# Group 3's keys and queries through TensorE instead of the DMA crossbar, and two loads issued ahead of the index tables

## The chip, the cores and the metric

The kernel runs on one core of a Trainium2 chip. The metric is the device time of one execution in microseconds (us); the kernel before takes 244.34 us (median of 3 runs, 244.31 to 244.9). The profile is one further execution, whose span from the first to the last instruction is 242.5 us.

The engines are named as in the profile: PE is TensorE (PEld its weight load), DVE is VectorE, ACT is ScalarE, POOL is GpSimd, SP is SyncE. POOLq and SPq stand for the issuing of transfers from these engines.

## The reference

Attention with a sliding window and sink positions, then a gated feed-forward block on its output. Four batches, eight heads, 768 positions, head size 64; each query sees itself, the 127 positions before it, and the first four positions (the sinks).

```python
scores = scale * np.matmul(q, k.transpose(0, 1, 3, 2))
keep = is_sink | in_window            # is_sink: pos < 4; in_window: 0 <= rel < 128
scores = np.where(keep, scores, -1000000000.0)
a = softmax(scores)                   # written out in the original
attn_out = np.matmul(a, v)
x = attn_out.transpose(0, 2, 1, 3).reshape(3072, 512)
g = x @ w_gate                        # 512 x 1536
silu = g * (1.0 / (1.0 + np.exp(-g)))
out = (silu * (x @ w_val)) @ w_out    # 1536 x 512
```

## The kernel before

The 3072 positions are cut into 12 groups of 256 (three groups in a batch). For each group keys and queries have to be brought from rows by position to columns by position (feature on partitions)[...]. The kernel does that in three ways: groups 0 and 1 by matmuls on specially packed rows, group 2 by TensorE transposes (`step_TN`), groups 3 to 11 by the DMA crossbar (`xbar`), from the queue of SyncE:

```python
rowp = pool("rowp", 3)
natp = pool("natp", 1)
...
def load_nat(g):
    b, c = divmod(g, GC)
    x = (natp if g > 2 else rowp).tile(
        [P, 2, 2, DM], BF16, tag="nat" if g > 2 else "rows", name="nat")
    for i, src in ((0, k), (1, q)):
        for j in range(2):
            t0 = c * 256 + j * P
            nc.gpsimd.dma_start(
                x[:, i, j].rearrange("p (h d) -> p h d", d=D),
                src[b, :, t0:t0 + P].rearrange("h p d -> p h d"))
    nats[g] = x
...
def step_TN(g, i, j):
    ...
    pt = bank([P, NP2, P], BF16, "pn")
    for p in range(NP2):
        nc.tensor.transpose(pt[:, p], nats[g][:, i, j, p * P:(p + 1) * P], ident)
    ...
    if i == 0:
        nc.scalar.copy(out=dst, in_=pt)
    else:
        nc.vector.tensor_copy(out=dst, in_=pt)

def xbar(g):
    ...
    for j in range(2):
        for i in range(2):
            t0 = c * 256 + j * P
            nc.sync.dma_start_transpose(
                (kTs, qTs)[i][b][:, :, t0:t0 + P], nats[g][:, i, j])
```

From group 3 on the blocks share `natp`, which holds one buffer: a group's block can be loaded only when the crossbar has read the one before it. The pool `rowp` has three buffers; the two fp32 staging tiles of the start and group 1's rows take them first.

GpSimd issues all loads of keys, queries, values and weights, in this order (cut):

```python
nc.gpsimd.iota(tq, ...)      # index tables: 0..127 along a row
nc.gpsimd.iota(tk, ...)      # 0..127 down the partitions
nc.gpsimd.iota(th8, ...)
for i in range(2):
    nc.gpsimd.dma_start(x0[:, i, 4:8], by_two((k, q)[i], 4))
load_rows(1)
load_v(0)
load_gate(0)
...                          # gates 1 and 2, values 1, group 2's block, gate 3, values 2, gates 4, 5
for i in range(4):
    load_out(i)
...
load_nat(3)
load_v(3)
```

Attention work is woven into the feed-forward work of the groups before it. `gate` projects with both weight matrices (`pg`, `pv`), `down` with the output weights (`pd`); a slot number says at which gate or down step an attention step stands, after `pg` and before `pv`. This is the first stage (slots 0 to 17 are gates, 18 to 23 downs):

```python
(11, [A(xbar, 3)]), (11, [NV(4)]),
(15, [A(xbar, 4)]), (15, [NV(5)]), (19, [A(xbar, 5)]), (19, [NV(6)]),
(23, [A(xbar, 6)]), (23, [NV(7)]),
((17, 18), Ss(3)), (18, [A(step_ks, 1)]), (18, [A(step_vsb, 1)]),
((19, 19, 19, 20), PVs(3)), (20, Xs(3)),
((19, 20), Ss(4)), (19, [K(4)]),
((21, 21, 22, 22), PVs(4)), (22, Xs(4))))
```

`NV(g)` loads group g's block and values, `Ss` computes scores, exponentials and masks, `K` the scores against the sinks, `PVs` the products with the values, `Xs` brings the normalised rows (`xn`) into columns (`xT`) for the gates: for groups 0, 1, 2 and 4 by TensorE, for the others by the crossbar.

At the start VectorE makes the identity and the masks from the index tables, before its first casts:

```python
nc.vector.tensor_scalar(ident, tq, tk, None, op0=ALU.is_equal)
...                                          # two halves of mask
nc.vector.tensor_scalar(sk, tk, float(NS), None, op0=ALU.is_lt)
...                                          # mask0: mask with the sinks let through
nc.vector.tensor_scalar(lt8, th8, float(NS), None, op0=ALU.is_lt)
...                                          # diag_h: which row belongs to which head's sinks
```

Of the kernel before, what the change touches and what calls it, by code (L numbers as in the profile page):

```python
# [8 lines left out]
BF16 = mybir.dt.bfloat16  # L9
AF = mybir.ActivationFunctionType  # L10
ALU = mybir.AluOpType
# [3 lines left out]
def kernel(  # L15
# [12 lines left out]
    nc = tc.nc  # L28
    P = 128
    B, H, S, D = q.shape  # L30
    NS = int(n_sink)
    W = int(window)
    DM = moe_w_gate.shape[0]
# [19 lines left out]
    def pool(name, bufs, psum=False):  # L53
        if psum:
            return ctx.enter_context(
                tc.tile_pool(name=name, bufs=bufs, space=bass.MemoryType.PSUM))
        return ctx.enter_context(tc.tile_pool(name=name, bufs=bufs))
# [3 lines left out]
    rowp = pool("rowp", 3)  # L61
    natp = pool("natp", 1)
# [15 lines left out]
    def bank(shape, dtype, name):  # L78
        return psum.tile(shape, dtype, tag="b", name=name)


    rows, nats, vas = {}, {}, {}

    def by_rows(src, b, w, pairs, t0):

        hs = slice(2 * pairs.start + w, 2 * pairs.stop, 2)
        return src[b, hs, t0:t0 + 256].rearrange("p (m r) d -> m p (r d)", r=4)
# [3 lines left out]
    def new_rows(g):  # L91
        rows[g] = rowp.tile([P, 2, NP2, 4 * D], BF16, tag="rows", name="rows")
        return rows[g]

    def load_rows(g):
        b, c = divmod(g, GC)
        x = new_rows(g)
        for i in range(2):
            for w in range(2):
                nc.gpsimd.dma_start(  # L100
                    x[64 * w:64 * (w + 1), i],
                    by_rows((k, q)[i], b, w, ALL, c * 256))

    def load_nat(g):
        b, c = divmod(g, GC)
        x = (natp if g > 2 else rowp).tile(
            [P, 2, 2, DM], BF16, tag="nat" if g > 2 else "rows", name="nat")
        for i, src in ((0, k), (1, q)):
            for j in range(2):
                t0 = c * 256 + j * P  # L110
# [5 lines that stand above are left out]
    def load_v(g):  # L116
        b, c = divmod(g, GC)
        va = vpool.tile([P, 2, H, VS], BF16, tag=f"va{g}", name="va")
        nc.vector.memset(va[:, :, :, D:D + 1], 1.0)
# [3 lines that stand above are left out]
                va[:, j, :, 0:D], v[b, :, t0:t0 + P].rearrange("h p d -> p h d"))  # L123
        vas[g] = va
# [3 lines left out]
    def load_gate(i, which=(0, 1)):  # L128
        f0, n = sum(FCH[:i]) * P, FCH[i] * P
        both = (wgs, moe_w_gate, "wg"), (wvs, moe_w_val, "wv")  # L130
        for lst, w, nm in (both[x] for x in which):
            t = wpool.tile([P, DMC, n], BF16, tag=f"{nm}{i}", name=nm)
            nc.gpsimd.dma_start(  # L133
                t, w[:, f0:f0 + n].rearrange("(c p) f -> p c f", p=P))
            lst.append(t)
# [9 lines left out]
    mask = const.tile([P, 2, 256], BF16)  # L145
    mask0 = const.tile([P, 2, 256], BF16)
    diag_h = const.tile([P, 4], BF16)
    vcf = const.tile([P, B, D + 1], FP32)
    tq = const.tile([P, P], FP32)
    tk = const.tile([P, 1], FP32)  # L150
    th8 = const.tile([P, 4, 4], FP32)
    lt8 = const.tile([P, 4, 4], FP32)
    sk = const.tile([P, 1], FP32)
# [15 lines left out]
    def by_two(src, h0):  # L169
        return src[0, h0:h0 + 4, 0:256].rearrange("h (m r) d -> m h (r d)", r=2)  # L170

    x0 = const.tile([P, 2, H, 2 * D], BF16)
# [5 lines left out]
    for h in range(H):  # L178
        r = 32 * (h // 4) + NS * (h % 4)
        nc.sync.dma_start(  # L180
            vcf[r:r + NS, :, 0:D], v[:, h, 0:NS].rearrange("b s d -> s b d"))
    nc.gpsimd.iota(tq, [[1, P]], base=0, channel_multiplier=0,
                   allow_small_or_imprecise_dtypes=True)
    nc.gpsimd.iota(tk, [[0, 1]], base=0, channel_multiplier=1,
                   allow_small_or_imprecise_dtypes=True)
    nc.gpsimd.iota(th8, [[-32, 4], [-NS, 4]], base=0, channel_multiplier=1,
                   allow_small_or_imprecise_dtypes=True)
    for i in range(2):
        nc.gpsimd.dma_start(x0[:, i, 4:8], by_two((k, q)[i], 4))
    load_rows(1)  # L190
    load_v(0)
    load_gate(0)
    load_gate(1, (0,))
    load_v(1)
# [8 lines left out]
    for i in range(4):  # L203
# [3 lines left out]
    tq2 = tq.rearrange("p (o x) -> p o x", o=1).broadcast_to([P, 2, P])  # L207
    nc.vector.tensor_scalar(mask[:, :, 0:P], tq2, tk, None, op0=ALU.is_lt)
    nc.vector.tensor_scalar(mask[:, :, P:2 * P], tq2, tk, None, op0=ALU.is_ge)
    nc.vector.tensor_scalar(sk, tk, float(NS), None, op0=ALU.is_lt)  # L210
    flat, flat0 = (m.rearrange("p a x -> p (a x)") for m in (mask, mask0))
    nc.vector.tensor_scalar(flat0[:, P:3 * P], flat[:, P:3 * P], sk, None, op0=ALU.max)
    nc.vector.tensor_copy(out=flat0[:, 3 * P:4 * P], in_=flat[:, 3 * P:4 * P])

    nc.vector.tensor_scalar(lt8, th8, float(NS), None, op0=ALU.is_lt)
    nc.vector.scalar_tensor_tensor(lt8, th8, 0.0, lt8, op0=ALU.is_ge, op1=ALU.mult)
    nc.vector.tensor_reduce(diag_h, lt8.rearrange("p q h -> p h q"), mybir.AxisListType.X,
                            op=ALU.max)

    kTs, qTs, es_t, e_t, xns, xTs = {}, {}, {}, {}, {}, {}  # L220
    later = []
# [1 line left out]
    def flush():  # L223
        for f in later:
            f()
        later.clear()

    def new_T(b):
        if b not in kTs:
            kTs[b] = kqtp.tile([P, NP2, S], BF16, tag="kT", name="kT")  # L230
            qTs[b] = kqtp.tile([P, NP2, S], BF16, tag="qT", name="qT")
# [17 lines left out]
        else:  # L249
            nc.vector.tensor_copy(out=dst, in_=pt)  # L250

    def step_TN(g, i, j):

        b, c = divmod(g, GC)
        new_T(b)
        pt = bank([P, NP2, P], BF16, "pn")
        for p in range(NP2):
            nc.tensor.transpose(pt[:, p], nats[g][:, i, j, p * P:(p + 1) * P], ident)
        t0 = c * 256 + j * P
        dst = (kTs, qTs)[i][b][:, :, t0:t0 + P]  # L260
        if i == 0:
            nc.scalar.copy(out=dst, in_=pt)
        else:
            nc.vector.tensor_copy(out=dst, in_=pt)
# [10 lines left out]
    def step_ks(b):  # L275
        for h in range(2):
            r = slice(h * D, (h + 1) * D)
            nc.vector.tensor_copy(
                out=kss[r, b, :, h * NS:(h + 1) * NS], in_=kTs[b][r, :, 0:NS])
# [204 lines left out]
    def A(fn, *a):  # L484
        return lambda: fn(*a)

    def TN(g):
        return [A(step_TN, g, i, j) for j in range(2) for i in range(2)]

    def Ss(g):  # L490
        return [A(step_S, g, p2) for p2 in range(2)]
# [42 lines left out]
    def pair_T(p):  # L534
        new_T(0)
        for i, dst in ((0, kTs[0]), (1, qTs[0])):
            pt = bank([P, 256], FP32, "pt")
            for r in range(2):
                for w in range(2):
                    nc.tensor.matmul(  # L540
                        pt[64 * w:64 * (w + 1), r:256:2],
                        x0[:, i, 2 * p + w, r * D:(r + 1) * D], ident,
                        start=True, stop=True, skip_group_check=True)
            if p < 2 and i == 0:
                nc.scalar.copy(out=dst[:, p, 0:256], in_=pt)
            else:
                nc.vector.tensor_copy(out=dst[:, p, 0:256], in_=pt)

    def pair_S(p, n=0):
        if p == 0:  # L550
            e_t[0] = epool.tile([P, H, 512], BF16, tag="e", name="e")
        pss = [bank([P, 512], FP32, "s") for _ in range(2)]
        fill(n, pss[0])
        for kk, n, col in ((0, 256, P), (P, P, 3 * P)):
            for h in range(2):
                r = slice(h * D, (h + 1) * D)
                nc.tensor.matmul(
                    pss[h][:, col:col + n], kTs[0][r, p, kk:kk + P],
                    qTs[0][r, p, kk:kk + n], start=True, stop=True)
        for h in range(2):  # L560
            nc.scalar.activation(
                e_t[0][:, 2 * p + h, P:512], pss[h][:, P:512], AF.Exp, scale=scale)
# [8 lines left out]
        cast(i, p)  # L571
    pair_T(0)
    pair_T(1)
    pair_S(0, 1)
    pair_S(1)
    pair_T(2)
# [17 lines left out]
    step_X(0, 0)  # L594
    step_X(0, 1)
    flush()
    step_ks(0)
    step_vsb(0)
    step_S(1, 1)
    later[:0] = masks1  # L600
    flush()
    load_nat(3)
    load_v(3)

# [5 lines left out]
    def L(*fs):  # L610
        def f():
            for x in fs:
                x()
        return f

    def NV(g):
        return L(A(load_nat, g), A(load_v, g))
# [4 lines left out]
        ((4, 4, 5, 5), TN(2)), ((6, 7), Ss(2)), (6, [K(2)]),  # L622
        ((8, 8), PVs(2)[:2]), (9, [A(step_PV, 2, 0, 1, "a"), A(step_PV, 2, 1, 1, "a")]),
        ((10, 11), [A(step_X, 2, 0, "a"), A(step_X, 2, 1, "a")]),
        (11, [A(xbar, 3)]), (11, [NV(4)]),
        (15, [A(xbar, 4)]), (15, [NV(5)]), (19, [A(xbar, 5)]), (19, [NV(6)]),
        (23, [A(xbar, 6)]), (23, [NV(7)]),
        ((17, 18), Ss(3)), (18, [A(step_ks, 1)]), (18, [A(step_vsb, 1)]),
# [59 lines left out]
```

## Time and profile before

| what | value |
|---|---|
| time | 244.34 us |
| span of the profiled execution | 242.5 us |
| PE busy | 231.7 us (96%) |
| DVE busy | 157.9 us (65%) |
| ACT busy | 113.0 us (47%) |
| POOL busy | 73.2 us (30%) |
| PE clock granted | full, in all slices |

"Busy" is the time in which at least one instruction of the engine ran. The row of slices in the profile cuts the span into 40 equal pieces of 6.06 us and gives the busy share of each in tenths. Which engine waited for whom is in the list of waits (total us, number of waits, longest). The chain of work is followed back from the last instruction to what released each step.

### The profile page before, as it was taken

To read this page: it belongs to the slowest core of one execution; us is meant where nothing else is said; L and a number is where in the kernel's file an instruction comes from. 1 tells how busy PE (TensorE), PEld (TensorE's weight loads), DVE (VectorE), ACT (ScalarE), POOL (GpSimd) and SP (SyncE) were. 2 spreads that over 40 slices of the span, in tenths; PEclk is the share of its full clock that TensorE was granted. 3 is DMA by queue.
4 is the path that set the end of the run, shared out by engine and by line. 5 is a ranking of instruction groups with operands and counts; after the bars stand their busy time and mean duration, and the time that the engine had idled before them with its cause. 6 is when DMAs were issued, how large, how long until landed. Compare 5 with 4: busy or idle time off the path is not lost.

```text
span 242.5 us, 4972 instructions
## 1 busy us (share of the span) xinstructions
PE 231.7 (96%) x1936; PEld 132.4 (55%) x1936; DVE 157.9 (65%) x336; ACT 113.0 (47%) x233; POOL 73.2 (30%) x94
## 2 busy tenths in 40 slices
PE   8999999999698899999999999999999999999994
PEld 5667979884344344444445454445454445488443
DVE  5798788778343498981497992388981398877100
ACT  4886495345451564522665612655512662233112
POOL 8986863043444308062080800053000000000000
PEclk9999999999999999999999999999999999999999
DMA  7999999969899999989799994569504200200132
GB/s 127 173 185 175 183 201 200 151 76 139 119 134 170 213 161 76 143 85 191 158 112 151 94 81 124 116 91 146 91 0 130 89 0 0 46 0 0 46 131 86
DMA packets 109767, 27.88 MB, mean 115 GB/s; under 512 B 96816, under 2 KB 106800, under 8 KB 109744
## 3 DMA queue, kind: packets, MB, share of 16 engines
q0 software_dynamic: 76640, 13.90, 77.1%
q1 hardware_dynamic: 32576, 13.41, 28.2%
q8 instruction: 15, 0.25, 0.4%
q10 hardware_dynamic: 528, 0.26, 0.4%
q14 instruction: 8, 0.07, 0.1%
HBM read 28.34 MB, written 6.29 MB: 143 GB/s over the span
## 4 chain that ended last, share of the span: by engine, by line
PE 73%; DMA 18%; SPq 2%; DVE 2%; POOL 2%; issue 2%; ACT 1%; POOLq 0%; DVEq 0%
PE pd L467 23%; PE pv L436 20%; PE pg L436 19%; DMA wv<-in_moe_w_val_dram 7%; DMA nat<-in_q_dram 6%; PE o L368 3%; PE s L305 3%; DMA qT<-nat 2%; SPq L272 2%; DMA xT<-xn 2%; PE w L524 2%; POOL nat L111 1%; PE pt L540 1%; PE pt L243 1%; PE o L348 1%
## 5 line engine op out<-in xcount | busy, mean ns | idle before, releaser
L436 PE MATMUL pg<-xT,wg 128*128 128x256 bf16 (+1 forms) x384 | 74.2, 326 | 2.8 <-DMA xT<-xn 2.1
L436 PE MATMUL pv<-xT,wv 128*128 128x256 bf16 (+1 forms) x384 | 74.3, 326 | 0.4 <-DVE xn L382 0.2
L443 ACT ACTIVATE th<-pg 128x512 f32<-128x512 f32 x72 | 43.4, 603 | 66.0 <-PE pg L436 65.6
L449 DVE SCALAR_TENSOR_TENSOR u<-th,pg 128x512 bf16<-128x512 f32 x72 | 49.2, 683 | 37.9 <-ACT th L443 37.9
L467 PE MATMUL pd<-wo,ht 128*128 128x512 bf16 (+1 forms) x300 | 66.2, 371 | 0.0
L450 DVE TENSOR_TENSOR ht<-u,pv 128x512 bf16<-128x512 bf16 x72 | 49.5, 688 | 10.9 <-PE pv L436 4.4
L436 PEld LDWEIGHTS <-wg 128*128 128x128 bf16 x384 | 37.2, 98 | 29.3 <-issue 3.9
L312 ACT ACTIVATE e<-s 128x512 bf16<-128x512 f32 (+1 forms) x88 | 42.8, 580 | 6.3 <-PE s L305 6.2
L436 PEld LDWEIGHTS <-wv 128*128 128x128 bf16 x384 | 34.4, 98 | 19.9 <-issue 1.7
L467 PEld LDWEIGHTS <-ht 128*128 128x128 bf16 x300 | 28.1, 98 | 28.7 <-issue 0.5
L111 POOL DMA_DIRECT2D nat<-in_k_dram x20 | 17.6, 886 | 85.4 <-DMA qT<-nat 82.7
L471 ACT ACTIVATE ot<-pd 128x512 f32<-128x512 f32 (+1 forms) x25 | 14.6, 583 | 48.4 <-PE pd L467 48.4
L317 DVE TENSOR_TENSOR e<-e,mask 128x1024 bf16<-128x1024 bf16 (+1 forms) x44 | 26.9, 649 | 6.3 <-ACT e L312 6.3
L122 POOL DMA_DIRECT2D va<-in_v_dram x24 | 21.6, 926 | 4.1 <-DMA wo<-in_moe_w_out_dram 2.5
L368 PEld LDWEIGHTS <-e 128*128 128x128 bf16 x352 | 15.4, 98 | 8.0
L382 DVE TENSOR_TENSOR xn<-o,rcp 128x256 bf16<-128x256 f32 x44 | 18.7, 425 | 1.5
L111 POOL DMA_DIRECT2D nat<-in_q_dram x20 | 17.7, 902 | 0.7 <-DMA wv<-in_moe_w_val_dram 0.5
L368 PE MATMUL o<-va,e 128*128 128x65 bf16 x352 | 17.4, 193 | 0.0
L305 PE MATMUL s<-qT,kT 64*128 64x128 bf16 (+1 forms) x240 | 13.4, 237 | 2.7 <-DMA qT<-nat 2.5
L305 PEld LDWEIGHTS <-kT 64*128 64x128 bf16 x240 | 7.8, 94 | 10.3 <-issue 7.3
L376 DVE RECIPROCAL rcp<-o 128x4 f32<-128x4 f32 x48 | 8.2, 176 | 5.7 <-PE o L368 5.6
L133 POOL DMA_DIRECT2D wv<-in_moe_w_val_dram x6 | 4.9, 810 | 0.5 <-DMA wv<-in_moe_w_val_dram 0.5
(65 smaller groups left out, 78.7 us busy)
## 6 DMA issues: line engine op xcount, KB each, us to landing
out_dram<-ot SPq DMA_DIRECT2D x23, 256.0 KB
va<-in_v_dram POOLq DMA_DIRECT2D x24, 128.0 KB, 6.1
nat<-in_k_dram POOLq DMA_DIRECT2D x20, 128.0 KB, 3.8
nat<-in_q_dram POOLq DMA_DIRECT2D x20, 128.0 KB, 5.2
wg<-in_moe_w_gate_dram POOLq DMA_DIRECT2D x6, 256.0 KB, 8.1
wv<-in_moe_w_val_dram POOLq DMA_DIRECT2D x6, 256.0 KB, 8.5
wo<-in_moe_w_out_dram POOLq DMA_DIRECT2D x4, 384.0 KB, 11.4
kT<-nat SPq DMA_TRANSPOSE x18
```

The source lines that it names most:

```text
L111: nc.gpsimd.dma_start(x[:, i, j].rearrange("p (h d) -> p h d", d=D), src[b, :, t0:t0 + P].rearrange("h p d -> p h d"))
L122: nc.gpsimd.dma_start(va[:, j, :, 0:D], v[b, :, t0:t0 + P].rearrange("h p d -> p h d"))
L305: nc.tensor.matmul(pss[2 * pp + h][:, col:col + n], kTs[b][r, p, kk:kk + P], qTs[b][r, p, qq:qq + n], start=True, stop=True)
L312: nc.scalar.activation(e_t[g][:, h0 + h, lo:512], pss[2 * pp + h][:, lo:512], AF.Exp, scale=scale)
L317: nc.vector.tensor_tensor(e, e, m[:, :, lo:512].broadcast_to([P, 2, 512 - lo]), op=ALU.mult)
L368: nc.tensor.matmul(o, l, r, start=(c == 0 and i == 0), stop=(i == len(mms) - 1), skip_group_check=True)
L382: nc.vector.tensor_tensor(xn, po[:, :, 0:D], rcp.broadcast_to([P, 4, D]), op=ALU.mult)
L436: nc.tensor.matmul(ps[:, i * n:(i + 1) * n], ws[fi][:, c, fo * P:(fo + 1) * P], x[:, c], start=(c == 0), stop=(c == DMC - 1))
L443: nc.scalar.activation(th, pg, AF.Tanh, scale=0.5)
L449: nc.vector.scalar_tensor_tensor(u, th, 1.0, pg, op0=ALU.add, op1=ALU.mult)
L450: nc.vector.tensor_tensor(hts[tb][:, f:f + two].rearrange("p a n -> p (a n)"), u, pv, op=ALU.mult)
L467: nc.tensor.matmul(po, hts[tb][:, f, ts * P:(ts + 1) * P], wos[f // n][:, f % n, lo:hi], start=(f == 0), stop=(f == DFC - 1))
```

## The change

Three things. Group 3's keys and queries are transposed on TensorE, in gate steps 14 and 15, and all four results are copied out by ScalarE (`"aa"`); its block is loaded into the three-buffer pool. The single buffer then holds group 4's block first, so that group 4 need not wait for group 3. Second, GpSimd issues the first two loads ahead of the index tables, and the third table only after the first values. Third, the mask with the sinks and the selection of sinks are made later on VectorE, where they are first needed.

```diff
-        x = (natp if g > 2 else rowp).tile(
-            [P, 2, 2, DM], BF16, tag="nat" if g > 2 else "rows", name="nat")
+        x = (natp if g > 3 else rowp).tile(
+            [P, 2, 2, DM], BF16, tag="nat" if g > 3 else "rows", name="nat")
...
+    for i in range(2):
+        nc.gpsimd.dma_start(x0[:, i, 4:8], by_two((k, q)[i], 4))
     nc.gpsimd.iota(tq, ...)
     nc.gpsimd.iota(tk, ...)
+    load_rows(1)
+    load_v(0)
     nc.gpsimd.iota(th8, ...)
-    for i in range(2):
-        nc.gpsimd.dma_start(x0[:, i, 4:8], by_two((k, q)[i], 4))
-    load_rows(1)
-    load_v(0)
     load_gate(0)
...
-    nc.vector.tensor_scalar(sk, ...)          # and mask0: now after pair_T(1)
-    nc.vector.tensor_scalar(lt8, ...)         # and diag_h: now after step_X(0, 1), before step_ks(0)
...
-    def step_TN(g, i, j):
+    def step_TN(g, i, j, evict="av"):
...
-        if i == 0:
+        if evict[i] == "a":
             nc.scalar.copy(out=dst, in_=pt)
...
-        (11, [A(xbar, 3)]), (11, [NV(4)]),
+        (11, [NV(4)]), ((14, 14, 15, 15), TN(3, "aa")),
```

More of the change, by code (lines that the diff above doesn't have):

```diff
@@ L209 @@
     nc.vector.tensor_scalar(mask[:, :, P:2 * P], tq2, tk, None, op0=ALU.is_ge)
[L210 to L218, printed above, removed]
     kTs, qTs, es_t, e_t, xns, xTs = {}, {}, {}, {}, {}, {}
@@ L485, in A, with TN @@
         return lambda: fn(*a)
-    def TN(g):
-        return [A(step_TN, g, i, j) for j in range(2) for i in range(2)]
+    def TN(g, evict="av"):
+        return [A(step_TN, g, i, j, evict) for j in range(2) for i in range(2)]
     def Ss(g):
@@ L573 @@
     pair_T(1)
+    nc.vector.tensor_scalar(sk, tk, float(NS), None, op0=ALU.is_lt)
+    flat, flat0 = (m.rearrange("p a x -> p (a x)") for m in (mask, mask0))
+    nc.vector.tensor_scalar(flat0[:, P:3 * P], flat[:, P:3 * P], sk, None, op0=ALU.max)
+    nc.vector.tensor_copy(out=flat0[:, 3 * P:4 * P], in_=flat[:, 3 * P:4 * P])
     pair_S(0, 1)
@@ L596 @@
     flush()
+    nc.vector.tensor_scalar(lt8, th8, float(NS), None, op0=ALU.is_lt)
+    nc.vector.scalar_tensor_tensor(lt8, th8, 0.0, lt8, op0=ALU.is_ge, op1=ALU.mult)
+    nc.vector.tensor_reduce(diag_h, lt8.rearrange("p q h -> p h q"), mybir.AxisListType.X,
+                            op=ALU.max)
     step_ks(0)
```

## The prediction

> **What bounds the kernel now.** I read four views: the page's row of slices, the waits of TensorE, the chain that ended last, and the timelines of the DMA queue and of TensorE around the stage that the chain points at. The first two:
>
> ```profile
> PE   8999999999698899999999999999999999999994
> DMA  7999999969899999989799994569504200200132
> ...
> PE s L305 <- DMA qT<-nat: 2.5, 2, 1.9
> PE pg L436 <- DMA xT<-xn: 2.1, 1, 2.1
> ```
>
> TensorE is busy for 231.7 of 242.5 us, so 10.8 us are idle. Slice 11 (60.6 to 66.7 us) is a 6, and slices 13 and 14 are 8s. The waits name the cause: the scores of a group wait for transposed queries (two waits, 2.5 us) and a gate projection waits for transposed activations (one wait, 2.1 us). Every other wait of TensorE is at most 1.1 us. The same by stretches (columns: stretch, its length, then busy time and count of TensorE, weight loads, VectorE, ScalarE, GpSimd, clock, DMA share, GB/s):
>
> ```profile
> 26.00:50.00 24.00, 23.87 (x273) 20.50 (x271) 19.27 (x37) 13.99 (x32) 9.10 (x12) 1.00 1.62 180
> 50.00:60.00 10.00, 10.00 (x93) 6.59 (x92) 8.26 (x19) 5.56 (x12) 5.26 (x6) 1.00 1.46 101
> 60.00:80.00 20.00, 15.43 (x141) 7.50 (x138) 7.49 (x20) 7.07 (x14) 9.43 (x11) 1.00 1.42 144
> ```
>
> From 60 to 80 us TensorE loses 4.57 us; from 26 to 60 it loses 0.13. So that stretch holds the large removable idle time. The chain says what stands behind it (start, us, what):
>
> ```profile
> 34.47 11.58 DMA nat<-in_q_dram
> 46.07 1.19 SPq L272
> 47.35 1.22 SPq L272
> 48.66 2.44 DMA qT<-nat
> 51.16 0.50 issue
> 51.67 1.73 POOL nat L111 x2
> 53.40 3.74 DMA nat<-in_q_dram
> 57.16 1.19 SPq L272
> 58.44 1.22 SPq L272
> 59.75 3.49 DMA qT<-nat
> 63.28 0.56 PE s L305 x10
> ```
>
> Group 3's block lands (46.05), the crossbar transposes it (until about 51.1), only then does GpSimd load group 4's block into the same single buffer (51.67), the crossbar transposes that (until 63.24), and group 4's scores start at 63.28. The queue of SyncE shows how it goes on:
>
> ```profile
> 67.37 1.50 SPq L272 DMA_TRANSPOSE kT<-nat  x1
> 70.12 1.19 SPq L272 DMA_TRANSPOSE qT<-nat  x1
> 71.41 1.22 SPq L272 DMA_TRANSPOSE kT<-nat  x1
> 72.72 1.22 SPq L272 DMA_TRANSPOSE qT<-nat  x1
> 74.02 0.53 SPq L472 DMA_DIRECT2D out_dram<-ot  x1
> 74.66 2.53 SPq L401 DMA_TRANSPOSE xT<-xn  x2
> ```
>
> These are group 5's transposes, pushed back by the same single buffer. Group 3's activations stand behind them in that queue. VectorE has finished them by about 67.0 (the product at 66.56 takes 0.42), but the transposes start at 74.66, the data is there at 79.9, and the gate at 80.02 has waited 2.08 us. Both waits have one root: group 3 and group 4 share the buffer.
>
> **What the Trainium skill says.** "TensorE: Matmul & The Clock Gate", section "Part 4: PE-mode transpose": a transpose is a matmul against an identity, does 128x128 at once, ends in PSUM and has to be copied out; about 275 ns in a kernel. The trace agrees in kind: group 2's sixteen transposes take 219 ns each from start to modelled end, but they overlap, and eight of them move the next matmul by only 0.45 us. "DMA: Bandwidth & Descriptors", section "DMA Transpose (X-bar)": a plain DMA transpose can only be issued by SyncE or ScalarE. Here all 52 stand in SyncE's one queue, which is why group 5 holds up group 3's activations. "Perfetto Trace Analysis", section "DMA Instruction — SWDGE (GPSIMD)": a GpSimd load's bar is descriptor generation, not data. The trace agrees: the bar is 0.88 us, the landing 3.3 to 12.5 us after issue. So I time loads by who waits for them.
>
> **The change, part by part.**
>
> *Removed:* group 3's four crossbar transposes (44.15 to 51.1) and the dependence of group 4's load on them. Group 3's block moves into the three-buffer pool, in a buffer that the fp32 staging gave up in the first microseconds; group 4's is now the first user of the single buffer. In the built program group 4's first load waits only for the load eight before it, as every GpSimd load in this stretch does. Worked out: the value loads of group 3 went out at 37.79 and 40.12, each when one of the four output-weight transfers had landed, some 2.3 us apart. The next two landings should be near 42.4 and 44.7, then group 3's keys near 44.1 and 45. So group 4's four loads issue at about 42 to 46, not 51.67 to 55.2. They queue behind two value blocks; I put their landing at 49 to 53. The transposes, 1.3 us apart plus 3.5 us for the last, end at 56 to 58 against 63.24.
>
> *What that is worth:* with the wait gone, group 4's scores are wanted at 60.55 (62.48 less its 1.93 of waiting), some 0.9 later with the transposes added below, so at 61.4. That leaves more than 3 us of margin. Both pieces of that wait go: 1.93 + 0.58 = 2.51 us. Group 5's block then loads at about 57 to 61, and its transposes leave SyncE by about 66. Group 3's activations start through the crossbar at about 66 to 68 instead of 74.66. With the 5.2 us that they took from first start to last landing they are in place by 73, while the gate wants them at about 76. So the 2.08 us go too. Sum: 4.59 us.
>
> *Added:* sixteen transposes on TensorE, eight each in the 15th and the 16th of this stage's 18 gate pairs, at the rate of group 2:
>
> ```profile
> 28.38 0.61 PE L258 MATMUL pn<-ident,nat 128*128 128x128 bf16 x8
> 28.82 1.04 PE L436 MATMUL pv<-xT,wv 128*128 128x256 bf16 x8
> ```
>
> 0.44 us per eight, so 0.9 us, in a stretch where TensorE has no gaps: paid in full. They come at about 48.2 and 50.3. Their data is there: keys at 44.15, queries at 46.05, and the second half no later than 48.66, when its transpose is started before. The four copies out go to ScalarE, 0.58 us each (two in a row about 1.07), into gaps of 1.15 us that it has before every tanh there, each gap now 0.44 longer: hidden, and VectorE gets nothing.
>
> *Moved, start:* the two loads take 0.90 and 0.75 us of GpSimd, so the tables that stood at 0.84 come at about 2.5 to 2.9. VectorE then makes identity and masks in about 0.95 us, until near 3.9. The identity is first used at 4.80, and VectorE's next work is the cast at 4.36, which waits for data. So it costs nothing, with 0.5 us to spare. The loads come 0.56 us earlier, but TensorE does not wait for them at 7.51. Gain: 0. The sink-row mask (three operations, about 0.5 us by their starts from 2.63 to 3.12) goes into VectorE's 0.78 us of waiting before 7.96: hidden.
>
> *Moved, sink selection:* three small operations (3.12 to 3.71, about 0.55 us) now stand ahead of group 1's masks at about 15.0. There VectorE has no gap until 22.58, and its reciprocals release ScalarE's normalisation (19.69 to 21.43), group 1's transposes (21.75) and the gate at 23.57, which already waits 0.31 us for ScalarE. About 0.3 us of the 0.55 is absorbed by slack in between (the transposes start 0.3 us after their input); I charge 0.2.
>
> *Sum:* 244.34 - 2.51 - 2.08 + 0.89 + 0.2 = 240.8 us, 1.4% less.
>
> **Rivals.** First, *only the first wait goes*. If group 4's block lands late (DMA is nine tenths busy up to 48.5 us, by slices 2 to 8), group 5 is still late and group 3's activations still wait behind it. For it speaks the 11.58 us that group 3's queries took; against it, that long landing came from weights queued ahead, which have drained by 44. It would give 244.34 - 2.51 + 1.1 = 242.9. Second, *TensorE's added work waits*: if the second half of group 3's block lands after 50, or a PSUM bank is not free, TensorE stalls in a stretch that had 0.13 us of idle time. Against it speaks that before, the crossbar had started on that half at 48.66. It would cost 1 to 2 us and give about 242. Third, *the start becomes the bound*: tables 1.7 us later, identity late, or the earlier loads slowing the staged halves that land at 4.36 and 4.76. Everything behind shifts by that. The margin is 0.5 us for the cast and 1.4 for the identity; a miss costs 0.3 to 1 us. Fourth, *more is gained than I count*: other idle time of TensorE is 1.1 us at the very start, about 3 in the end tail, and under 0.3 at a time elsewhere; none of it depends on this buffer. Hence 239.45 (2% less) is hard to reach: it needs 4.9 us, and the two waits together are 4.6 before costs.
>
> **Range and chances.** The sum is 240.8; I put the prediction at 240.9. Below, the added cost can at best be zero: 239.9 would be nearly the full 4.59. Above, the first rival and half of the third stay within 242.7. Faster by over 2%: 0.06. Slower by over 2% would need 4.9 us of new waits, for which I see no source: 0.02. Within 2%: 0.92.
>
> **What would show it.** In the changed profile, TensorE's wait for transposed queries and its wait for transposed activations should be gone from the list, and the stretch between 60 and 80 us should lose under 0.5 us. Group 4's loads should issue before 47 us, its transposes end before 59, and group 3's activations start through the crossbar before 69. The new transposes should be two groups of eight of 0.44 us without idle time before them. The first transposes of the pairs should start near 4.8 as before, and the fourth gate pair near 23.8. I am wrong if a wait on group 3's block or on the identity appears, or if the activations' wait stays.

## The result and the profile after

The changed kernel takes 240.94 us (median of 6 runs, 240.43 to 241.69); the kernel before, beside it, 244.64 (244.31 to 246.01). The ratio is 0.984, with a 95% interval of 0.981 to 0.987. The profiled execution has a span of 239.5 us against 242.5.

The same views of the changed kernel. From the page, the busy tenths of TensorE and of the DMA engines in 40 slices; then what TensorE waited for (total us, number, longest; what is left out is at most 0.3 us each):

```profile
PE   8998999999999999999999999999999999999994
DMA  8999999993999999799699984699504200200122
```

```profile
PE w L515 <- DVE one L162: 1.1, 1, 1.1
PE pv L427 <- DMA wv<-in_moe_w_val_dram: 0.7, 1, 0.7
PE pg L427 <- DVE u L440: 0.5, 1, 0.5
...
```

The 6 and the two 8s in the middle of TensorE's row are gone, and so are both waits: for transposed queries (2.5 us) and for transposed activations (2.1). Two small ones are new: 0.7 us for a value weight near 23 us and 0.5 us for VectorE near 137 us. By stretches (columns as before):

```profile
50.00:60.00 10.00, 10.00 (x90) 7.07 (x89) 7.55 (x15) 6.81 (x16) 1.88 (x3) 1.00 0.95 86
60.00:80.00 20.00, 20.00 (x191) 10.09 (x190) 10.11 (x28) 9.74 (x20) 8.62 (x10) 1.00 1.57 170
```

From 60 to 80 us TensorE is never idle, where it lost 4.57 us. The timelines of GpSimd's loads and of SyncE's transfers show how:

```profile
42.19 0.87 POOL L111 DMA_DIRECT2D nat<-in_k_dram  x1 [0.60 <-DMA wo<-in_moe_w_out_dram]
44.11 0.88 POOL L111 DMA_DIRECT2D nat<-in_k_dram  x1 [1.05 <-DMA wo<-in_moe_w_out_dram]
45.02 1.85 POOL L111 DMA_DIRECT2D nat<-in_q_dram  x2
...
58.12 1.75 POOL L111 DMA_DIRECT2D nat<-in_k_dram  x2 [9.40 <-DMA qT<-nat]
```

```profile
50.24 1.29 SPq L263 DMA_TRANSPOSE kT<-nat  x1
...
55.14 1.22 SPq L263 DMA_TRANSPOSE qT<-nat  x1
...
70.09 2.53 SPq L392 DMA_TRANSPOSE xT<-xn  x2
```

Group 4's four loads issue from 42.19 (before: 51.67), its transposes from 50.24, and they have landed before group 5's load, which waits for them, starts at 58.12. Group 3's activations enter the queue at 70.09 instead of 74.66. And on TensorE, the new transposes:

```profile
48.84 0.61 PE L249 MATMUL pn<-ident,nat 128*128 128x128 bf16 x8
49.29 1.04 PE L427 MATMUL pv<-xT,wv 128*128 128x256 bf16 x8
50.16 1.04 PE L427 MATMUL pg<-xT,wg 128*128 128x256 bf16 x8
51.04 0.61 PE L249 MATMUL pn<-ident,nat 128*128 128x128 bf16 x8
```

They start without idle time before them, and eight of them move what follows by 0.45 us. The next table shows where the 3.0 us between the two spans come from, read from when the same TensorE instruction starts in both timelines. A stage is here one of the eight blocks of rows that the kernel works through (three of 256 rows, four of 512, one of 256); the fourth takes the activations of groups 3 and 4, the fifth those of groups 5 and 6.

| instruction | before | after | shift | change of the shift, and its cause |
|---|---|---|---|---|
| fourth gate pair | 23.57 | 24.24 | +0.67 | +0.67, a value weight landed later |
| group 3's first scores | 53.50 | 55.07 | +1.57 | +0.90, the sixteen transposes |
| down step after group 4's first scores | 63.78 | 62.60 | -1.18 | -2.75, first wait gone |
| fourth stage's first gate | 80.02 | 76.60 | -3.42 | -2.24, second wait gone |
| fifth stage's first gate | 116.65 | 112.85 | -3.80 | -0.38, of which 0.23 less waiting for VectorE |
| sixth stage's first gate | 153.85 | 150.54 | -3.31 | +0.49, a wait for VectorE (0.48 at 137.72) |
| last 84 down matmuls | 223.67 | 220.36 | -3.31 | 0, no new loss to here |

The tail from the last matmuls to the end is 0.3 us longer after the change, which leaves 3.0. The medians differ by more, 3.70 us: the profiled execution of the kernel before took 244.31 us and that of the changed one 241.3, by 0.33 below and 0.36 above their medians.

### The profile page after: what moved, and what is told of

The parts are those of the page before. It is cut to its first block, busy times and chain, and to the rows that moved or that the text cites. A ratio compares the mean times of both kernels' runs of the same rounds, so it can differ in the third digit from the quotient of the medians.

```text
span 239.5 us, 4998 instructions
## 1 busy us (share of the span) xinstructions
PE 232.2 (97%) x1952; PEld 133.4 (56%) x1952; DVE 158.6 (66%) x336; ACT 114.6 (48%) x237; POOL 73.2 (31%) x94
## 4 chain that ended last, share of the span: by engine, by line
PE 84%; POOL 5%; DMA 4%; DVE 3%; issue 1%; ACT 1%; POOLq 0%; DVEq 0%; ACTq 0%
PE pd L458 26%; PE pv L427 24%; PE pg L427 24%; DMA wv<-in_moe_w_val_dram 4%; PE s L296 4%; PE o L359 4%; POOL va L122 1%; POOL rows L100 1%; DVE u L440 1%; PE pn L249 1%; POOL x L183 1%; POOL wg L133 1%; DVE ht L441 1%; POOL wv L133 1%; PE pk L324 1%
```

## Experiments

Theory: the two waits came from one buffer shared by groups 3 and 4; the gain is the waits less 0.9 us of transposes, and the new start is worth next to nothing. Rivals: the crossbar and the traffic on the DMA engines, not the buffer, were the limit; or the start costs what the table's first line shows. All ratios are against the kernel before, run beside them; on the chips of these experiments that kernel took 246.5 to 246.9 us (median). Each is the kernel before with the named edit alone, unless said otherwise.

**The first part without the new start.** Group 3 on TensorE and in the three-buffer pool; loads, index tables and masks in their old order.

```diff
-        x = (natp if g > 2 else rowp).tile(
+        x = (natp if g > 3 else rowp).tile(
...                                    # tag likewise; step_TN with evict
-        (11, [A(xbar, 3)]), (11, [NV(4)]),
+        (11, [NV(4)]), ((14, 14, 15, 15), TN(3, "aa")),
```

> The kernel before with only the first part of the change: group 3 transposed on TensorE and its block in the three-buffer pool; the start (order of loads, identity, masks, sink selection) as before. If the whole gain comes from this part and the new start costs about 0.67 us (the fourth gate pair stands at 24.24 instead of 23.57 in the changed profile), this is 240.2 to 240.4, faster than the changed kernel by 0.5 to 0.7, with the fourth gate pair at about 23.6. If the late weights at the start are only chance of one execution, it is 240.9 like the changed kernel.

Measured: 241.59 us, ratio 0.9795 (0.9763 to 0.9826). The whole gain is in this part. Its fourth gate pair stands at 23.53.

**The new start alone.** The order of loads and tables, and the later mask and sink selection.

> The kernel before with only the new start: two loads ahead of the index tables, third table after the first values, mask with sinks and sink selection later. If the new start costs 0.67 us on the path and the stalls at 60 to 80 us then absorb none of it or part of it, 244.6 to 245.3: what it delays on TensorE can be hidden in the wait for group 4's queries, which depends on the loads. If GpSimd's loads all come 0.4 us later, that wait moves along with them and the full amount stays (245.2). If the start helps, below 244.4.

Measured: 246.43 us, ratio 0.998 (0.9954 to 1.0006): no difference that can be told. In its profile the first gate stands at 14.71 instead of 15.19, but the next gates then wait 0.42 us for a value weight, and the fourth pair is at 23.58, where it was (23.57). That the start itself is quicker is not shown: the first gate moves between 14.83 and 15.19 in the profiles with the old start.

**The buffer alone.** Group 3 still goes through the crossbar.

```diff
-        x = (natp if g > 2 else rowp).tile(
+        x = (natp if g > 3 else rowp).tile(
...                                    # tag likewise
```

> The kernel before with one line changed: group 3's block in the three-buffer pool, and still transposed by the crossbar. If the shared single buffer alone made both waits, both go here too, without the 0.9 us of transposes on TensorE and without the new start: 244.6 - 4.9 = 239.7 (239.4 to 240.2), faster than the changed kernel by about 1. If the crossbar and SyncE's queue were what held group 4 up (eight transposes of 1.3 us one after another, then group 3's activations behind them), a wait of 1 to 3 us stays and it is 241 to 243.

Measured: 245.91 us, ratio 0.9994 (0.9973 to 1.0016). The theory fails: no gain can be told. Its chain of waits (start, us, what):

```profile
34.78 11.60 DMA nat<-in_q_dram
...
48.99 9.00 DMA qT<-nat
58.95 1.82 PE pv L436 x8
```

Group 3's last transpose issues at 48.99, as before (48.66), but lands 9.00 us later, not 2.44. What is different is that group 4's loads, issued from 41.86 on, are now under way beside it, and that group 4's own transposes follow in the queue from 50.45. TensorE waits 4.29 us, now for group 3's own queries, and afterwards its clock is low:

```profile
55.00:60.00 5.00, 1.87 (x14) 1.24 (x15) 0.19 (x1) 1.36 (x4) 0.00 (x0) 0.67 1.39 127
60.00:65.00 5.00, 4.78 (x23) 2.02 (x23) 2.99 (x6) 1.92 (x5) 3.38 (x4) 0.65 0.56 37
```

The clock column reads 0.67 and 0.65 where the kernel before has 1.00. "DMA: Bandwidth & Descriptors" of the Trainium skill, section "Issuing engines are not separate DMA queues", says that transfers started by ScalarE, SyncE or GpSimd run on the same 16 DMA engines and interleave. The two numbers for the same transpose, 2.44 and 9.00, agree with that.

**TensorE alone.** Group 3 transposed on TensorE, its block still in the single buffer; group 4's load is put after the transposes that free it.

```diff
...                                    # step_TN with evict
-        (11, [A(xbar, 3)]), (11, [NV(4)]),
+        ((14, 14, 15, 15), TN(3, "aa")), (15, [NV(4)]),
```

> The kernel before with group 3 transposed on TensorE, but its block still in the single buffer, so that group 4's block loads only after TensorE has read it (about 51 us). If the buffer is the cause, the waits stay near 2.5 and 2 us, less what TensorE arrives later by: 243.5 to 244.8, with group 4's first load issued at 50 to 52. If it was the crossbar's time that mattered, the gain of the changed kernel shows here too: 240.5 to 241.5.

Measured: 245.19 us, ratio 0.9943 (0.9917 to 0.997). Group 4's load issues at 51.25, as in the kernel before, and the second wait stays (1.72 us); the first is 0.9 us, as TensorE comes later. So neither half carries the gain: the buffer alone gives nothing that can be told, TensorE alone 0.6%, both 2.1%.

**Extra traffic.** To test the collision by itself: four more loads of 128 KB behind group 3's values, into a tile that nothing reads. Buffers and order of the rest as before.

```diff
     load_v(3)
+    extra = const.tile([P, 2, 2, DM], BF16, tag="extra", name="extra")
+    ...        # four nc.gpsimd.dma_start into extra, rows of batch 1
```

> The kernel before with four more loads of 128 KB (into a tile that nothing reads) issued right behind group 3's values, so that they run while the crossbar transposes group 3, as group 4's loads did in the buffer-only run. Buffers and waits are those of before. If loads in flight are what slows the crossbar, group 3's last transpose lands 4 to 7 us later than the 51.1 of before, TensorE waits 2 to 5 us for group 3's queries near 54, group 4 comes later by as much, and the ratio is 1.015 to 1.035. If the buffer-only result came from something else (order of waits, the pool), group 3's transposes land near 51 and the ratio is below 1.005.

Measured: 249.11 us, ratio 1.0115 (1.0079 to 1.0151), less than expected. The chain:

```profile
48.81 6.18 DMA qT<-nat
...
55.54 1.74 POOL nat L111 x2
```

and on TensorE:

```profile
55.12 0.51 PE L305 MATMUL s<-qT,kT 64*128 64x256 bf16 x8 [1.15 <-DMA qT<-nat]
...
65.77 0.23 PE L305 MATMUL s<-qT,kT 64*128 64x128 bf16 x2 [3.59 <-DMA qT<-nat]
```

The last transpose lands 6.18 us after issue (2.44 before), with group 3's and 4's buffer as it was, and group 4's load moves from 51.67 to 55.54. In four profiles without the extra loads (the kernel before, the new start alone, and two runs below) that load stands between 51.67 and 51.78. TensorE waits 5.4 us for queries in all, but only 1.15 us of it for group 3's, less than the 2 to 5 expected; the rest is for group 4's, which come later because the buffer is freed later. That loads in flight slow the crossbar's transposes is shown. The 9.00 us of the buffer-only run had two more loads beside it and group 4's transposes behind it; how much each of these added is not shown.

**Group 3's loads ahead of the output weights.** The buffer-only kernel with that change of order, so that group 3's transposes come before group 4's loads.

```diff
+    load_nat(3)
+    load_v(3)
     for i in range(4):
         load_out(i)
...
-    load_nat(3)
-    load_v(3)
```

> The kernel with group 3's block in the three-buffer pool and still on the crossbar, as in the buffer-only run, but its loads issued ahead of the four output weights. In the buffer-only run group 3's last transpose took 9.0 us from issue to landing while group 4's loads ran beside it (2.44 in the kernel before). If that collision is what ate the gain, here group 3's transposes are done before the scores want them at 53.5, and the time falls by 4 to 5 us against before (ratio 0.980 to 0.984), as no transposes are on TensorE. If crossbar transposes are slow beside any loads, the output weights now do the same harm: a wait of 2 to 5 us for group 3's queries stays, and the ratio is 0.99 to 1.0.

Measured: 243.59 us, ratio 0.9883 (0.9825 to 0.994): between the two expectations. The wait for queries is gone, since group 3's transposes run from 36.72. But group 4's block, issued at 38.82 behind the output weights, is first used by the crossbar at 53.44; group 5 is late as before, and group 3's activations enter at 73.01 and make TensorE wait 3.42 us. Half of the gain comes with group 3 still on the crossbar (1.2%, against 2.2% for the changed kernel on the same chip).

**Group 5 behind group 3's activations** in SyncE's queue.

```diff
-        (19, [A(xbar, 5)]), (19, [NV(6)]),
+        (20, [A(xbar, 5)]), (20, [NV(6)]),     # after Xs(3)
```

> The kernel before with group 5's four transposes put into SyncE's queue behind group 3's activations instead of ahead of them; nothing else. If the second wait is the order in that queue (late transposes of group 5 in front), it goes and the first stays: 2.0 to 2.2 us less than before (ratio 0.991 to 0.992). If the activations were late for another reason (their own transposes slow, or vector work), the wait stays near 2 and the time is that of before.

Measured: 245.84 us, ratio 0.9953 (0.9915 to 0.9991). The profile is of an execution longer than the median (249.82 us, span 248.0) and is read for the order of events only. The activations enter the queue at 66.91, and the fourth stage's gate starts without a wait: the place in the queue was the cause of the second wait. But there is a new wait of 3.71 us one stage later. The chain there:

```profile
111.74 7.74 DMA xT<-xn
...
119.52 1.89 PE pg L436 x4
```

Group 6's activations take 7.74 us, next to loads issued from 106.91. In this execution the time won by order is given back at the next transfer. Whether the others have the new wait is not shown; their gain, 0.5%, is less than the 0.8 to 0.9% expected.

**Group 3's activations on TensorE** in the kernel before (`PEX = (0, 1, 2, 3, 4)`).

> The kernel before, with group 3's activations brought into columns by TensorE instead of the crossbar; nothing else. It takes the second wait away (2.1 us in the profile of before) at 0.45 us for eight transposes on TensorE; the first wait stays. If the two waits are two separate losses, the fourth stage's gate starts 1.6 us earlier and the ratio is 0.993 or a little less. If the time is given back at the next crossbar transfer, as in the run with group 5 behind the activations, the ratio is 0.995 to 1.0.

Measured: 244.51 us, ratio 0.9893 (0.9824 to 0.9962). The first wait stays (2.4 us in its two pieces), the second is gone, and a wait of 0.68 us for activations appears one stage later, at 115.86. The second wait alone is worth about 1% here (0.4 to 1.8% by the interval), about half of the change.

**The changed kernel again, and without its new start,** on one chip.

> The changed kernel itself, on this chip beside the others. If the new start is free on average, ratio equal to that of the run below within 0.2%; if the 0.67 us by which the fourth gate pair was later in its profile is a cost of the new start, 0.25% above it. On the chip of the first experiments the kernel before was slower (246.7 us), so both should stand at 0.98 if that holds here.

> The change without its new start, for the direct comparison with the changed kernel on one chip. Same as the changed kernel within 0.2% if the start is bound by the arrival of the gate weights, which both have alike; 0.25% below it if the new start costs 0.67 us.

Measured: 241.00 us, ratio 0.9779 (0.973 to 0.9828), and 241.02 us, ratio 0.9787 (0.9738 to 0.9836). The new start is worth nothing that can be measured. The fourth gate pair stands at 23.86 and 23.41 here, at 24.24 in the first profile of the change and at 23.84 in the buffer-only run, which has the old start: its place moves from execution to execution.

**The changed kernel with group 3's activations on TensorE too.**

> The changed kernel with group 3's activations also by TensorE. What is left of the second wait there is 0 to 0.3 us in two profiles (0.7 and 0.8 with the old start), the transposes cost 0.45: same as the changed kernel within 0.3%, slightly slower if anything, unless the two fewer crossbar transposes let later transfers land earlier.

Measured: 241.87 us, ratio 0.9821 (0.9769 to 0.9873), not distinguishable from the change (0.9779 on another chip). The waits of 0.3 and 0.8 us that the expectation counts as left of the second wait stand one stage later, at 113 us, in the profiles of the two runs above; in both the fourth stage's first gate does not wait. No version was found that beats it.

## Why the prediction was right, and where not

The time (240.9 predicted, 240.94 measured) was right, and the waits that the sum counts did go. That the two agree to 0.04 us is in part luck: the sum starts from 244.34, while the kernel before had a median of 244.64 beside the change, and the two profiles differ by 3.0 us where the sum has 3.5. On the chips of the experiments the gain was larger, 5.1 us without the new start and 5.9 for the change itself. The sum has no term for that; the last section says what goes with it. Point by point:

- **First wait.** Predicted 2.51 us gone; 2.75 went. The issue of group 4's loads (42 to 46 predicted; 42.19 to 46.9) and the end of its transposes (56 to 58; before 58.12) were right.
- **Second wait.** Predicted 2.08 us gone; 2.24 went in the first profile. But the margin was misjudged: the activations entered the queue at 70.09, not at 66 to 68, because the transpose of group 5's queries came at 64.78, three microseconds after that of its keys (61.47), and the last one left SyncE at 69.37, not at about 66. In the profile without the new start 0.36 us of the wait was left. In three profiles waits for activations of 0.29 us (change), 0.35 and 0.83 us (old start) stand one stage later, near 113 us, where the kernel before has none.
- **Transposes on TensorE.** Predicted 0.89 us, paid in full; 0.90. ScalarE took the copies (0.58 and 0.61 us) in its gaps.
- **Start.** Predicted +0.2 for the sink selection. It did delay VectorE (the first gate product moved from 18.10 to 19.07, more than the 0.55 worked out), but two runs on one chip differ by 0.02 us, so no cost can be measured. Why not is not shown. TensorE waits 0.67 us for the third value weight in the first profile of the change, but not in the second, and in the second the later wait for activations is shorter than with the old start (0.29 against 0.83 us).
- **The root.** This is the step that failed, although it left the sum right: "Both waits have one root: group 3 and group 4 share the buffer." The buffer-only run shows that freeing the buffer gives nothing that can be told (ratio 0.9994) as long as group 3 stays on the crossbar, because group 4's earlier loads then slow group 3's transposes from 2.44 to 9.00 us (6.18 with extra loads and the buffers unchanged). The sum gave nothing to the four removed crossbar transposes. They are what makes the earlier loads harmless. In the changed kernel no crossbar transpose is in flight until 50.24, when the first of those loads has arrived.
- **Rivals.** That only the first wait goes did not happen. The late second half did not happen. That the start becomes the bound did not happen: the wait for a value weight near 23 us also stands in profiles with the old start (0.42, 0.60 and 0.99 us). That more is gained than counted did not happen beside the first result (1.6%), but did on the chips of the experiments (2.1 to 2.2%).

## What to carry to other kernels

Before freeing a buffer so that a load can start earlier, list what else is on the DMA engines at that time: a crossbar transpose that landed 2.4 us after its issue in one order landed 6 to 9 us after it beside more loads, and the wait only changed its name. Moving a transpose to TensorE may pay not for its own time but because it leaves the DMA engines to the loads. A wait removed by reordering a queue is worth what the next transfer in that queue leaves of it.

## What was not expected of the hardware

TensorE's clock fell to 0.50 for some microseconds after some of its waits, and stayed at 1.00 after others of like length. With group 3's activations on TensorE in the changed kernel, in an execution of 244.45 us, a wait of 1.98 us for a gate weight was followed by this (the second line is a stretch as above):

```profile
22.59 1.55 PE L427 MATMUL pg<-xT,wg 128*128 128x256 bf16 x8 [1.98 <-DMA wg<-in_moe_w_gate_dram]
24.00:25.00 1.00, 1.00 (x11) 0.94 (x10) 0.20 (x1) 0.83 (x2) 0.98 (x2) 0.50 1.63 187
```

and with the new start alone, a wait of 2.92 us by this:

```profile
80.91 1.02 PE L426 MATMUL pg<-xT,wg 128*128 128x512 bf16 x4 [2.92 <-DMA xT<-xn]
80.00:85.00 5.00, 4.09 (x35) 1.91 (x36) 1.98 (x4) 3.03 (x7) 1.36 (x2) 1.00 1.79 242
```

Summed over stretches of 1 us, the clock was at half for about 3.4 us after the 1.98 us and after 3.42 us with group 3's loads moved ahead, and for about 6.8 us around or after 4.29 us in the buffer-only run and 3.59 and 0.65 us with the extra loads. The 1.93 and 2.08 us of the kernel before left it at 1.00. "TensorE: Matmul & The Clock Gate" of the Trainium skill, section "Why this matters for your kernels", advises against idle gaps above some 3 us between matmuls; these runs agree in part only, as 1.98 us was enough in one and 2.92 us was not in another. So the length of a wait alone does not decide, and what does is not shown. Where the clock falls, a wait costs more than it lasts: 3.4 us at half clock are 1.7 us of full-clock work (an estimate from these numbers).

This bears on the size of the gain. The mean clock of every execution of the experiments is on record, and 3.4 us at half clock lower the mean over 245 us by 0.007, twice that by 0.014 (estimates). Of the 19 executions of the kernel before beside the second runs of the change, three stand at 0.999 or 1.0 (median 245.4 us), eight at 0.992 or 0.993 (246.5 us), seven at 0.984 to 0.986 (247.7 us), and the longest, 249.7 us, at 0.978. The six of the changed kernel stand at 0.999 or 1.0 (240.06 to 241.19 us). So the spread of the kernel before, and the gain of 5.9 us where the first result has 3.7, go in part with the clock. That the two long waits bring the low clock about is likely but not shown, as none of these 19 executions has a profile.
